# Linear attention and a leaky-ReLU MLP on one core: product 4 of the output in seven quarter products

## The chip, the cores and the metric

The kernel runs on one core of a Trainium2 chip. A core has a matrix engine (TensorE, PE in the profile; its weight loads are listed apart as PEld), a vector engine (VectorE, DVE), a scalar engine (ScalarE, ACT) and GpSimd (POOL). Transfers are issued on the queues of SP, ACT and POOL. Each engine works through its own instructions in order and waits on semaphores for the others. The metric is the device time of one execution in microseconds (us); lower is better.

## What is computed

```python
kv  = einsum('bhsd,bhse->bhde', k, v)          # 8 batches, 8 heads, 576 tokens, head size 64
out = einsum('bhsd,bhde->bhse', q, kv)
x   = out / sqrt(mean(out**2, -1) + 1e-6) * g_norm     # then (4608 tokens) x (512)
h   = x @ w_in                                  # 512 -> 2048
g   = maximum(0.01 * h, h)
y   = g @ w_out                                 # 2048 -> 512
```

All is float32. Attention is a small part of the work. The two products of the MLP are most of it.

## The kernel before

**Blocks and pieces.** The 4608 tokens are 9 blocks of 512 (`NB`, index `i`). The 2048 hidden columns are 4 pieces of 512 (`NC`, index `c`). One pair (i, c), numbered n = (i-1)*4 + c, has two parts. Its h part computes the 512 x 512 piece of h for the block, which becomes g after the leaky ReLU. Its output part multiplies this piece of g by the matching 512 rows of `w_out` and adds the result to the block's output. Block 0 is computed plainly while the weights arrive, block 1 with one level of Strassen's method (Winograd's form), and blocks 2 to 8 as follows.

**Strassen's method in short.** A product of two matrices, each cut into four quadrants, is made of 7 products instead of 8. The operands are quadrants or sums of quadrants, and the results are added up. The kernel numbers the products 1 to 7. The order is `ORDER = (1, 2, 6, 5, 7, 3, 4)`. Products 1, 6, 7 and 4 follow one another in one PSUM bank and 2 (or 5) and 3 in another, each read out before the next is added on top.

**h, two levels (`product_h_two`).** Each of the 7 outer products (j) is itself made of 7 inner products (k) of 128 x 128 quarters. A step is one k for all seven j: 4 matmuls into bank `ha` or `hc`, 3 into `hb` or `hd`. Fresh results are copied by ACT into `qa` and `qc`, others added there by DVE. The first index of `qa[:, at, j, :]` is the quadrant that k belongs to, the second the outer product j. After the seventh step DVE adds up the outer products to the quadrants g11, g21, g22, g12 with seven instructions of 128x512 (lines 960 to 970), ACT applies `relu` to each, and POOL makes the sums that the output products 5, 6, 7 and 3 need (`sums_of`, four instructions of 128x512).

**Output, one level (`product_o`).** Seven products, each of 4 matmuls of 128x256 in program order. The profile shows two matmul records for each matmul, thus 8 records of 128x256 for an output product and 2 of 128x128 for a quarter. Product 2 of the indices 4 to 29 is not made here. It is made in seven quarter products by `Second`, one in each h step of index n+2, in the free fourth column of the bank `hb` or `hd`. For these indices `product_o` runs in the order `(1, 5, 6, None, 7, 3, 4)`, where None is a slot without an output step. Results are added to the output tiles `o11`, `o12`, `o21` and `o22` by DVE, or copied by ACT at the first piece of a block (c = 0). `finish` stores a tile when its last product of the block is in it.

**Slots.** An index has seven slots, t = 0 to 6; `slot = 7*c + t` counts through a block. The main loop writes into each slot, in this order: one step of h; steps of the attention of a later block (`FINE_SLOTS`, `LATE_SLOTS`); sums of the next block's x (`sums`, by DVE, in slots 20 to 22; `inner`, by POOL, in slots 24 and 25 and after 27); loads; the inner sums of g for `Second` (`inner_g`, POOL, at t = 4 and 6); and one step of the output product. The output steps of index n run two slots late (`LAG`): from t = 2 of index n+1 to t = 1 of index n+2. Blocks 2 to 8 keep this program order on each engine (`steady`), except for the relus, copies by ACT and stores, which a planner may place.

**Weights.** The quarters of `w_in` and their sums lie in DRAM (`w1_dram`) and pass through a ring of five places (`w_place`, `RING`), one load of 448 KB per slot on SP's queue (line 742). The sums of `w_out` for products 5 and 6 (`t12`) and 7 and 4 (`t34`) are loaded by the inner function `sums` of `sides_w2` on the same queue (line 674), 512 KB each, for index n+1 as soon as index n no longer needs the place.

**Lines that recur in the profile.** L118 is every matmul. L637 is every addition by DVE or POOL (`add`). L833 is `relu`. L952 is the copy of h by ACT, L1003 the copy of an output product. L400 and L402 scale x at the end of an attention, L455 turns q.

Of the kernel before, what the change touches and what calls it, by code (L numbers as in the profile page):

```python
# [9 lines left out]
F32 = mybir.dt.float32  # L10
# [13 lines left out]
def kernel(  # L24
# [36 lines left out]
    nc = tc.nc  # L61
    B, H, S, D = q.shape
    DM, DF = w_in.shape
    P = 128
# [34 lines left out]
    NW = U * NE * P  # L99
    w1_all = consts.tile([P, 2 * NC * NW], F32, name="w1_all")  # L100
    stage = consts.tile([P, 3 * NW], F32, name="stage")
    pairs = consts.tile([P, 4 * NW], F32, name="pairs")
    g_all = [consts.tile([P, 4 * U * N2], F32, name=f"g_{i}") for i in range(2)]

    def view(t, lo, *shape):
# [79 lines left out]
    zeros = view(g_all[0], 0, NT)  # L185
    nc.vector.memset(zeros[:, :64], 0.0)
    nc.vector.memset(zeros[:, 64:], 0.0)
    ident = consts.tile([P, P], F32, name="ident")

    def make_ident():  # L190
        pin(nc.gpsimd.memset(ident, 1.0))
# [449 lines left out]
    def sides_w1(c):  # L641
# [9 lines left out]
        def more():  # L651
# [5 lines left out]

    w2_dram = [[dram.tile([P, 2, U, N2], F32, name=f"w2_{c}_{i}") for i in range(2)]
               for c in range(NC)]
    t12, t34 = pair(2, 2, U, N2), pair(3, 2, U, N2)  # L660
    writes = []

    def sides_w2(n):

        c = n % NC
        b11, b12 = w2_sb[0][c][:, :, :N2], w2_sb[0][c][:, :, N2:]
        b21, b22 = w2_sb[1][c][:, :, :N2], w2_sb[1][c][:, :, N2:]

        def sums(i):
            t = (t12, t34)[i]
            if n >= NC:
                pin(nc.sync.dma_start(t, w2_dram[c][i]))
                return
            if i == 0:
                add(nc.gpsimd, t[:, 0], b12, b11, True)
                add(nc.gpsimd, t[:, 1], b22, t[:, 0], True)
            else:
                add(nc.gpsimd, t[:, 0], b22, b12, True)  # L680
                add(nc.gpsimd, t[:, 1], b21, t12[:, 1], True)
            if (n, i) == (NC - 1, 1):

                writes.append((w2_dram[c][i], t))
            else:
                pin(nc.sync.dma_start(w2_dram[c][i], t))
        return {1: b11, 2: b21, 3: b22, 5: t12[:, 0], 6: t12[:, 1], 7: t34[:, 0],
                4: t34[:, 1]}, sums
# [49 lines left out]
    def read(to):  # L738
        nonlocal n_read
        while n_read < min(to, len(reads)):  # L740
# [5 lines left out]
    qc = pair(0, 4, 3, P)  # L746
    xt1 = [work.tile([P, 2, N2], F32, tag="xt1", name="xt1"),
           view(w1_all, RING * NG + 24 * P, 2, N2)]
    xt24 = [work.tile([P, 2, 2, N2], F32, tag="xt24", name="xt24"),
            view(w1_all, RING * NG + 16 * P, 2, 2, N2)]  # L750
    xi = view(stage, 0, 3, 7, P)

    def sides_x(i):


        x = xTs.pop(i)
        b11, b12 = x[:, :2, :N2], x[:, :2, N2:]
        b21, b22 = x[:, 2:, :N2], x[:, 2:, N2:]
        home = i % 2 if i > 1 else 0
        t1, t2, t4 = xt1[home], xt24[home][:, 0], xt24[home][:, 1]  # L760
        if i == 1:
            t4 = opool.tile([P, 2, N2], F32, tag="o", name="xt4", bufs=6)
        t3 = b12
        sides = {1: b11, 2: b21, 3: b22, 4: t4, 5: t1, 6: t2, 7: t3}

        def sums():
            for t, a, b in ((t1, b12, b11), (t2, b22, t1), (t3, b22, b12), (t4, b21, t2)):
                add(nc.vector, t, a, b, True)
                yield

        batches, quarters, at = [], {k: {} for k in ORDER}, 0
        upper, lower = (x[:, h:h + 2, :].rearrange("p r (t v n) -> p t r v n", t=2, v=2)
                        for h in (0, 2))
        for js, y in (((1, 7), upper), ((2, 3), lower),
                      ((6, 4), xt24[home].rearrange("p t r (v n) -> p t r v n", v=2)),
                      ((5,), t1.rearrange("p r (v n) -> p r v n", v=2).unsqueeze(1))):
            terms = [y[:, :, r, v, :] for r in range(2) for v in range(2)]
            terms += [xi[:, k, at:at + len(js), :] for k in range(3)]
            batches.append(terms)
            for n, j in enumerate(js):  # L780
                for k, term in zip((1, 7, 2, 3, 5, 6, 4), terms):
                    quarters[k][j] = term[:, n, :]
            at += len(js)

        def inner(kind):
            for y11, y12, y21, y22, t1, t2, t4 in batches:
                if kind == 0:
                    add(nc.gpsimd, t1, y12, y11, True)
                    add(nc.gpsimd, t2, y22, t1, True)
                elif kind == 1:  # L790
                    add(nc.gpsimd, y12, y22, y12, True)
                else:
                    add(nc.gpsimd, t4, y21, t2, True)

        return sides, quarters, sums(), inner
# [83 lines left out]

    gi = view(pairs, 12 * P, 4, P)

    def inner_w2(c):
        y = w2_sb[1][c]
# [7 lines left out]

    def inner_g(c, half):

        g = g_of(c)[3]
        a11, a21, a12, a22 = (g[:, n, :] for n in range(4))
        s1, s2, s3, s4 = (gi[:, n, :] for n in range(4))
        if half == 0:
            add(nc.gpsimd, s1, a21, a22)  # L900
            add(nc.gpsimd, s2, s1, a11, True)
        else:
            add(nc.gpsimd, s3, a11, a21, True)
            add(nc.gpsimd, s4, a12, s2, True)

    class Second:
# [17 lines left out]
        def done(self, k, bank):  # L924
# [3 lines left out]
            if self.n % NC == NC - 1 and k == ORDER[-1]:  # L928
                self.finish("11", self.o)

    def product_h_two(i, c, quarters, to, second):

        n0 = 7 * ((i - 2) * NC + c)
# [1 line left out]
        into = {1: (0, True), 2: (0, False), 6: (1, True), 5: (3, True), 7: (3, False),  # L935
                3: (1, False), 4: (2, True)}
        banks = {}
        for t, k in enumerate(ORDER):
            for js, tags, q in zip(GROUPS, (("ha", "hc"), ("hb", "hd")), (qa, qc)):
                tag = tags[0 if k in (1, 6, 7, 4) else 1]  # L940
# [14 lines left out]
                if len(js) < 4 and second:  # L955
                    second.done(k, banks[tag][:, 3, :])
            read(n0 + t + 1 + RING)
            yield
        g11, g21, g22, g12 = g_of(c)
        add(nc.vector, g21, qa[:, :, 0, :], qa[:, :, 1, :])  # L960
        add(nc.vector, g11, qa[:, :, 0, :], qc[:, :, 0, :])
        yield
        add(nc.vector, g22, g21, qa[:, :, 2, :])
        add(nc.vector, g12, g22, qa[:, :, 3, :])
        yield
        add(nc.vector, g22, g22, qc[:, :, 1, :])
        yield
        add(nc.vector, g21, g21, qc[:, :, 1, :])
        add(nc.vector, g21, g21, qc[:, :, 2, :])
        for t in (g11, g12, g22, g21):  # L970
            relu(t)
        sums_of(c, to)

    def product_o(n, g_sides, os, finish, second):

        c = n % NC
        w_sides, _ = sides_w2(n)
        sums = sides_w2(n + 1)[1] if n + 1 < NC * (NB - 1) else lambda i: None
        if c == 0:

            for key in ("12", "22", "11", "21"):
                os[key] = opool.tile([P, 2, N2], F32, tag="o", name=f"o{key}", bufs=6)


        pieces = ((0, slice(0, N2)), (1, slice(0, P)), (1, slice(P, N2))) \
            if n + 1 == NC * (NB - 1) else None
# [2 lines left out]

        def done(i, bank):  # L990
            key, fresh = into[i]
            if isinstance(bank, list):
                for at, (end, (part, cols)) in enumerate(zip(bank, pieces)):
                    to = os[key][:, part, cols]
                    add(nc.vector, to, end, to)
                    if i == ORDER[-1]:
                        finish(key, os[key], part, cols, (nc.sync, nc.scalar)[at % 2])
                if i == 7:
                    finish(key, os[key])
                return  # L1000
# [2 lines left out]
                nc.scalar.copy(to, bank)  # L1003
            else:
                add(nc.vector, to, bank, to)
            if c == NC - 1 and i in (2, 7, 3, 4):
                finish(key, os[key])

            if i == (6 if second else 5):
                sums(0)  # L1010
            elif i == 4:
                sums(1)


        yield from strassen((("oa", "oc"), ("oc", "oa"))[n % 2], lambda i, part, r: g_sides[i][:, 2 * r + part, :],
                            lambda i, part, r: w_sides[i][:, r, :], done,
                           (1, 5, 6, None, 7, 3, 4) if second else ORDER,
                           pieces=pieces)

    def go(steps, n=None):  # L1020
        while n is None or n > 0:
# [16 lines left out]
    def first_block(between):  # L1038
# [26 lines left out]
                       start=(now[2] == 0), stop=(n == 2 * NC * U))  # L1065
            between(n, 1)
        for t in range(4):
            o = opool.tile([P, DM], F32, tag="o", name="o", bufs=6)
            if t % 2:
                nc.scalar.copy(o, accs[t])  # L1070
            else:
# [35 lines left out]
    for part in range(2):  # L1107
# [4 lines left out]
    FINE_SLOTS = {1: 1, 2: 1, 4: 1, 9: 1, 10: 2, 11: 1, 12: 1, 15: 1, 16: 2, 17: 2, 18: 1, 19: 1,  # L1112
                  23: 1, 24: 1, 25: 1, 26: 1}
    LATE_SLOTS = (3, 4)

    LAG = 2

# [1 line left out]
    HELD = (22, 24, 26)  # L1119
    o_queue, waited = collections.deque(), 0  # L1120

    seconds = {}

    def second_of(n):
        if n in seconds:
# [9 lines left out]
    for i in range(1, NB):  # L1135
# [4 lines left out]
        for c in range(NC):  # L1140
# [3 lines left out]
            for t in range(7):  # L1144
                slot = 7 * c + t
                go(h_steps, 1)
                if not one:

                    if t == 6:
                        go(h_steps, 1)  # L1150
                    if slot in LATE_SLOTS:
                        go(late, 1)
                    for _ in range(FINE_SLOTS.get(slot, 0)):
# [1 line left out]
                    if i + 1 < NB:  # L1155
                        if slot == 20:
                            x_sides, new_quarters, sums, inner = sides_x(i + 1)
                        if slot in (20, 21, 22):
                            go(sums, 2 if slot == 20 else 1)
                        if slot == 24:  # L1160
                            inner(0)
                        elif slot == 25:
                            inner(1)
                    load_some()

# [1 line left out]
                if now - 1 in seconds:  # L1167
# [2 lines left out]
                            inner_g((now - 1) % NC, half)  # L1170
                    if t == 5 and now <= 2 * NC:
                        inner_w2((now - 1) % NC)
                if slot == 4 and not one:
                    while writes:
                        pin(nc.sync.dma_start(*writes.pop()))
# [32 lines left out]
            for _ in range(2 if i == NB - 1 and c == NC - 1 else 0):  # L1208
                go(h_steps, 1)
                go_o()  # L1210
            go(h_steps)
            if c == NC - 1 and i + 1 < NB:
                inner(2)
                quarters = new_quarters
# [39 lines left out]
```

## Time and profile before

| | us |
|---|---|
| median of 3 runs | 918.88 |
| runs | 918.8, 918.88, 924.28 |
| the profiled execution, device time | 917.78 |
| its span, first to last instruction | 916.1 |

| engine | what it does most | count, mean ns |
|---|---|---|
| PE | output product, 128x256, bank `o_a`, operands in `pairs` and `gs` | x384, 381 |
| PE | h, 128x128, bank `h_ha`, operands in `stage` and the weights | x448, 276 |
| DVE | output tile + bank `o_c`, 128x512 | x87, 684 |
| DVE | sum of g, 128x512 | x84, 689 |
| ACT | leaky ReLU, 128x512 | x124, 631 |
| POOL | sum of g for the output, 128x512 | x64, 1277 |
| POOL | inner sum of g, 128x128 | x52, 459 |

The mean of a matmul [...] overlaps the next one, so what a matmul costs is read from the distance between starts or from a stretch of many. DVE's instructions overlap a little in the same way. Times in a timeline are us from the start of the span. The granted clock of PE is 1.00 in every stretch.

### The profile page before, as it was taken

How to read it: one execution, taken by the hardware profiler on the slowest of the kernel's cores; microseconds unless marked ns; L12 is line 12 of the kernel's file. 1: busy time of each engine (PE TensorE's matmuls, PEld its weight loads, DVE VectorE, ACT ScalarE, POOL GpSimd, SP SyncE). 2: the span in 40 equal slices, each digit the busy share in tenths (PEclk: the TensorE clock that was granted, in tenths of full speed). 3: DMA queues.
4: the chain of work that ended last, by engine and by line, in shares of the span. 5: the costliest groups of instructions: out<-in, count | busy, mean ns of one | idle time of the engine just before them, and what ended most of it. 6: DMA issues, size and time to landing. Idle time of an engine off the chain costs nothing.

```text
span 916.1 us, 18037 instructions
## 1 busy us (share of the span) xinstructions
PE 909.3 (99%) x6980; PEld 776.3 (85%) x6980; DVE 631.6 (69%) x1168; ACT 328.2 (36%) x645; POOL 370.2 (40%) x438
## 2 busy tenths in 40 slices
PE   9999999999999999999999999999999999999998
PEld 5444448888998999899999999999999999999997
DVE  4876995587457876587756786678659755755565
ACT  5454533242135233533343324332343333223330
POOL 2000355967633473226421642264226422642222
DMA  8999926885599778776886789658765676667632
GB/s 269 236 245 249 248 85 191 280 285 167 166 360 289 228 209 268 233 230 214 255 247 230 219 249 272 222 178 212 242 183 176 187 222 198 185 185 223 197 109 92
DMA packets 90228, 200.05 MB, mean 218 GB/s; under 512 B 9888, under 2 KB 42272, under 8 KB 90144
## 3 DMA queue, kind: packets, MB, share of 16 engines
q1 hardware_dynamic: 79680, 187.04, 68.6%
q10 hardware_dynamic: 10016, 10.69, 3.4%
q8 instruction: 55, 0.90, 0.4%
q0 software_dynamic: 448, 1.18, 0.3%
q14 instruction: 29, 0.24, 0.1%
HBM read 172.39 MB, written 26.48 MB: 217 GB/s over the span
## 4 chain that ended last, share of the span: by engine, by line
PE 96%; DMA 2%; DVE 1%; issue 0%; ACT 0%; POOL 0%; SPq 0%; ACTq 0%; DVEq 0%; POOLq 0%
PE o_a L118 19%; PE o_c L118 18%; PE h_ha L118 11%; PE h_hb L118 11%; PE h_hc L118 8%; PE h_hd L118 8%; PE o_acc L118 6%; PE h_ps L118 6%; PE o_ps L118 3%; PE h_a L118 2%; PE h_b L118 1%; PE h_c L118 1%; PE h_d L118 1%; PE kv_ps L118 1%; DMA pairs<-in_v_dram 1%; DMA v_in<-in_v_dram 1%
## 5 line engine op out<-in xcount | busy, mean ns | idle before, releaser
L637 POOL TENSOR_TENSOR gs<-g 128x512 f32<-128x512 f32 x64 | 81.7, 1277 | 253.3 <-ACT g L833 253.3
L833 ACT ACTIVATE g<-g 128x512 f32<-128x512 f32 x124 | 78.2, 631 | 131.9 <-DVE g L637 131.9
L952 ACT COPY w_all<-h_ha 128x512 f32<-128x512 f32 x84 | 48.9, 582 | 173.5 <-PE h_ha L118 167.8
L118 PE MATMUL o_a<-pairs,gs 128*128 128x256 f32 x384 | 91.3, 381 | 0.0
L118 PE MATMUL o_c<-pairs,gs 128*128 128x256 f32 x376 | 89.2, 380 | 0.0
L637 DVE TENSOR_TENSOR o<-h_hb,o 128x128 f32<-128x128 f32 x104 | 29.8, 287 | 83.8 <-ACT pairs L952 83.7
L637 DVE TENSOR_TENSOR o<-o_c,o 128x512 f32<-128x512 f32 (+1 forms) x91 | 61.2, 672 | 23.9 <-PE o_c L118 23.6
L118 PEld LDWEIGHTS o_a<-pairs,gs 128*128 128x128 f32 x384 | 69.8, 190 | 9.2 <-POOL pairs L637 1.2
L118 PEld LDWEIGHTS o_c<-pairs,gs 128*128 128x128 f32 x376 | 68.3, 190 | 7.6
L637 DVE TENSOR_TENSOR o<-o_a,o 128x512 f32<-128x512 f32 x75 | 51.2, 683 | 28.2 <-PE o_a L118 28.1
L637 POOL TENSOR_TENSOR pairs<-w_all 128x512 f32<-128x512 f32 x8 | 11.1, 1384 | 120.6 <-ACT cut L245 102.3
L118 PE MATMUL h_ha<-stage,w_all 128*128 128x128 f32 x448 | 59.6, 276 | 0.0
L118 PEld LDWEIGHTS h_ha<-stage,w_all 128*128 128x128 f32 x448 | 56.6, 192 | 3.0 <-issue 0.7
L118 PE MATMUL h_ps<-xT,w_all 128*128 128x512 f32 (+1 forms) x136 | 58.0, 570 | 0.9 <-DVE w_all L258 0.9
L118 PE MATMUL o_acc<-w,g 128*128 128x512 f32 x128 | 57.8, 595 | 0.0
L637 DVE TENSOR_TENSOR g<-g,pairs 128x512 f32<-128x512 f32 x84 | 55.7, 689 | 1.9
L637 POOL TENSOR_TENSOR pairs<-g 128x128 f32<-128x128 f32 x52 | 23.9, 459 | 75.4 <-PE h_hb L118 46.7
L118 PEld LDWEIGHTS h_ps<-xT,w_all 128*128 128x128 f32 x136 | 25.5, 190 | 30.0 <-issue 26.6
L637 DVE TENSOR_TENSOR w_all<-h_hc,w_all 128x512 f32<-128x512 f32 x56 | 38.3, 684 | 15.9 <-PE h_hc L118 15.8
L118 PEld LDWEIGHTS o_acc<-w,g 128*128 128x128 f32 x128 | 24.0, 190 | 29.8 <-issue 29.4
L637 DVE TENSOR_TENSOR o<-h_hd,o 128x128 f32<-128x128 f32 x78 | 22.1, 283 | 37.8 <-ACT pairs L952 37.7
L118 PE MATMUL h_hb<-stage,w_all 128*128 128x128 f32 x336 | 46.7, 275 | 0.0
(228 smaller groups left out, 2264.6 us busy)
## 6 DMA issues: line engine op xcount, KB each, us to landing
w_all<-w SPq DMA_DIRECT2D x196, 448.0 KB, 4.2
pairs<-w SPq DMA_DIRECT2D x56, 512.0 KB, 4.3
out_dram<-o ACTq DMA_DIRECT2D x35, 256.0 KB, 4.6
v_in<-in_v_dram SPq DMA_DIRECT2D x29, 288.0 KB, 5.7
k_in<-in_k_dram SPq DMA_DIRECT2D x28, 288.0 KB, 5.1
q_in<-in_q_dram SPq DMA_DIRECT2D x56, 144.0 KB, 6.0
q_in<-in_q_dram SPq DMA_DIRECT2D x56, 140.0 KB, 5.8
w<-stage SPq DMA_DIRECT2D x12, 512.0 KB, 4.6
```

Source lines behind the costliest of these rows:

```text
L118: pin(nc.tensor.matmul(*args, **kw))
L637: ins = eng.tensor_tensor(out_, a, b_, op=ALU.subtract if minus else ALU.add)
L833: nc.scalar.activation(t, t if src is None else src, func=AF.Prelu, alpha=SLOPE)
L952: nc.scalar.copy(q[:, at], bank)
```

## The change

Product 4 of the output is made in seven quarter products for the indices n = 8 to 28 (`four(n)`), by a new class `Fourth`:

- `Fourth` makes its quarters in four steps at t = 1, 2, 3 and 4 of index n+2, right after the step of h: (1, 2, 5), (6, 3), (7) and (4). They go into three columns of the PSUM bank in which products 1, 6 and 7 of n were. Each quarter result is added to `o21` by DVE, or copied by ACT where it is the first of a block.
- Its operands are quarters of `w_out` sums that POOL makes once in block 2 (`inner_w4`) and that go to DRAM (`w4_dram`); for each index 256 KB and 192 KB are loaded in place of 256 KB. `inner_g` makes the inner sums for g12 (product 2) and g22 (product 4) together, 256 columns wide in place of 128.
- `product_o` of these indices runs in the order `(1, None, 6, 5, 7, 3, None)`. Product 7 goes to an output tile of its own ("7"), which is added to `o22` and to `o21` at the end of a block.
- The sums of g are made first for quadrant 0 (after the fourth step of h, at t = 3), the rest after the last step: four instructions at t = 6, and three with the relus and POOL's sums after the next index's first step of h (`h_rest`).
- The sums of x run in slots 20, 22, 23 and 25, one each, and POOL's inner sums of x in slots 26 and 27 and after.
- The tiles: `pairs` grows by 4*128 columns; the output tiles have 4 buffers, and 2 for `o11`, in place of 6; `ident` lies in the place of a later tile.

```diff
+        def sums(i, row=None):
             t = (t12, t34)[i]
+            if n >= NC and i:
+                if row != 1:
+                    pin(nc.sync.dma_start(t[:, 0], w2_dram[c][i][:, 0]))
+                if row == 0:
+                    return
+                if not four(n):
+                    pin(nc.sync.dma_start(t[:, 1], w2_dram[c][i][:, 1]))
+                    return
+                pin(nc.sync.dma_start(f4, w4_dram[c][:, :4, :]))
+                pin(nc.sync.dma_start(f4_more, w4_dram[c][:, 4:, :]))
+                return
...
+    class Fourth:
+        STEPS = (1, 2, 5), (6, 3), (7,), (4,)
+        COLUMN = {1: 0, 6: 0, 7: 0, 4: 0, 2: 1, 5: 2, 3: 2}
...
+        def step(self, at):
+            if at == 0:
+                self.bank = ps_m.tile([P, 4, P], F32, tag=self.tag, name=f"f_{self.tag}")
+            for k in self.STEPS[at]:
+                matmul(self.bank[:, self.COLUMN[k], :], lhsT=self.left[k], rhs=self.right[k],
+                       start=(k == 1), stop=True, skip_group_check=True)
+            for k in self.STEPS[at]:
+                bank = self.bank[:, self.COLUMN[k], :]
+                v, s = INTO[k]
+                to = self.o_of("21")[:, v, s * P:s * P + P]
+                if self.n % NC == 0 and k in (1, 5, 6, 4):
+                    nc.scalar.copy(to, bank)
+                else:
+                    add(nc.vector, to, bank, to)
+            if at == 3:
+                self.last()
...
+        def add_up(lo, hi):
+            g11, g21, g22, g12 = (g[:, lo:hi, :] for g in g_of(c))
+            a, b = qa[:, lo:hi], qc[:, lo:hi]
+            add(nc.vector, g21, a[:, :, 0, :], a[:, :, 1, :])
+            add(nc.vector, g11, a[:, :, 0, :], b[:, :, 0, :])
+            yield
+            add(nc.vector, g22, g21, a[:, :, 2, :])
+            add(nc.vector, g12, g22, a[:, :, 3, :])
+            yield
+            add(nc.vector, g22, g22, b[:, :, 1, :])
+            yield
+            add(nc.vector, g21, g21, b[:, :, 1, :])
+            add(nc.vector, g21, g21, b[:, :, 2, :])
...
             read(n0 + t + 1 + RING)
+            if t == 3:
+                for _ in add_up(0, 1):
+                    pass
             yield
...
+        for _ in add_up(1, 4):
+            yield
+        for g in g_of(c):
+            relu(g)
         sums_of(c, to)
...
+            if fourth and i == 7:
+                if c == NC - 1 or not four(n + 1):
+                    add(nc.vector, os["22"], os["22"], os["7"])
+                if c == NC - 1:
+                    finish("22", os["22"])
...
+            elif i == 4 and NC <= n < 2 * NC:
+                inner_w4()
+                later.extend(([3, lambda: (
+                    pin(nc.sync.dma_start(w4_dram[c][:, :4, :], f4)),
+                    pin(nc.sync.dma_start(w4_dram[c][:, 4:, :], f4_more)))],
+                    [4, lambda: sums(1, 1)]))
...
+        def last():
+            sums(1, 1)
+            if c == NC - 1 or not four(n + 1):
+                add(nc.vector, os["21"], os["21"], os["7"])
...
+        if fourth or four(n - 1):
+            order = (1, None, 6, 5, 7, 3, None if fourth else 4)
+        elif second:
+            order = (1, 5, 6, None, 7, 3, 4)
...
                     if t == 6:
-                        go(h_steps, 1)
+                        go(h_steps, 1 if (i, c) == (NB - 1, NC - 1) else 2)
+                    if t in FOURTH_AT and four((i - 1) * NC + c - 2):
+                        fourths[(i - 1) * NC + c - 2].step(t - FOURTH_AT[0])
+                    if t == 0:
+                        go(h_rest)
...
-                        if slot in (20, 21, 22):
-                            go(sums, 2 if slot == 20 else 1)
-                        if slot == 24:
+                        if slot in (20, 22, 23, 25):
+                            go(sums, 1)
+                        if slot == 26:
                             inner(0)
-                        elif slot == 25:
+                        elif slot == 27:
                             inner(1)
```

## The prediction

> **What bounds the kernel now.** I read the page's busy shares and its chain first. The chain is the work that ended last, followed back to the start.
>
> ```profile
> PE 909.3 (99%) x6980; PEld 776.3 (85%) x6980; DVE 631.6 (69%) x1168; ACT 328.2 (36%) x645; POOL 370.2 (40%) x438
> ...
> PE 96%; DMA 2%; DVE 1%; issue 0%; ACT 0%; POOL 0%; SPq 0%; ACTq 0%; DVEq 0%; POOLq 0%
> ```
>
> TensorE (PE) is never idle and is the chain. The time can fall only if PE has less to do, and it rises by whatever makes PE wait. Next come the stretches of one index n = (i-1)*4 + c (seven slots). The columns are stretch, length, then busy time of PE, PEld, DVE, ACT and POOL.
>
> ```profile
> 592.40:617.58 25.18, 25.18 (x250) 23.02 (x248) 20.33 (x39) 9.52 (x19) 15.30 (x20) 1.00 0.62 189
> 617.58:640.45 22.87, 22.87 (x162) 21.63 (x161) 18.91 (x34) 6.46 (x12) 10.23 (x12) 1.00 0.80 210
> ...
> 734.92:757.79 22.87, 22.87 (x162) 21.63 (x161) 11.59 (x24) 8.22 (x15) 6.83 (x8) 1.00 0.72 219
> ...
> 780.65:803.92 23.27, 23.13 (x161) 21.70 (x160) 17.13 (x31) 6.46 (x12) 15.07 (x20) 1.00 0.61 185
> ```
>
> These are n=19 (c=3), 20 (c=0), 25 and 27. A piece takes 22.87 us of pure PE work, more where attention adds matmuls. VectorE (DVE) fills 81-83% of a c=3 and a c=0 piece, but only half of n=25. Only n=27 loses something, 0.4 us. Two slots of n=20 price the matmuls:
>
> ```profile
> 631.63:635.14 3.51, 3.51 (x25) 3.31 (x24) 3.48 (x7) 0.00 (x0) 1.73 (x2) 1.00 0.92 189
> 635.14:636.93 1.79, 1.79 (x17) 1.78 (x16) 1.79 (x3) 0.00 (x0) 0.00 (x0) 1.00 1.05 340
> ```
>
> The second has only a step of h: 8 quarter products (16 records of 128x128), 1.79 us, so 0.224 us per quarter. The first has an output step besides, so a product of 8 records of 128x256 costs 3.51 - 1.79 = 1.72; the chain lists them at 1.73.
>
> [...] Here 1.73/8 = 0.216 against 1.79/16 = 0.112 us, 1.93: [...] so halving the width is nearly free and 7 for 8 is kept.
> [...] The trace has 689 and 283-287. Cutting one instruction in two costs DVE a fixed part.
> [...] POOL's 1.27 us sum from 599.03 holds a sum of x to 1.28, where 0.68 is usual, and POOL's next takes 1.61.
>
> ```profile
> 599.56 1.28 DVE L637 TENSOR_TENSOR xT<-xT 128x512 f32<-128x512 f32 x1
> ```
>
> **The change part by part.**
>
> *Product 4 (n = 8 to 28: 21 times).* Four matmuls of 128x256 go (1.73 us), seven quarters come (7 x 0.224 = 1.57). PE saves 0.16 x 21 = **3.4 us**. This is on the path.
>
> *Their evictions.* One DVE add of 128x512 becomes seven of 128x128. DVE starts back to back at these distances in n=20:
>
> ```profile
> 623.95 0.68 DVE L637 TENSOR_TENSOR o<-o_c,o 128x512 f32<-128x512 f32 x1
> 624.55 0.68 DVE L637 TENSOR_TENSOR w_all<-h_hc,w_all 128x512 f32<-128x512 f32 x1
> 625.15 0.55 DVE L637 TENSOR_TENSOR pairs<-h_hd,pairs 128x384 f32<-128x384 f32 x1
> 625.61 0.28 DVE L637 TENSOR_TENSOR o<-h_hd,o 128x128 f32<-128x128 f32 x1
> 625.81 1.25 DVE L455 STREAM_TRANSPOSE qT<-q_in 128x576 f32<-128x576 f32 x1
> ```
>
> That is 0.60, 0.46 and 0.20 us for 512, 384 and 128. So 7 x 0.20 - 0.60 = +0.8 us of DVE per index. Where n%4 is 0, four of them are ACT copies; ACT is 28-44% busy in these pieces and hides them. Product 7 now goes to a tile of its own, and two adds of 128x512 per block join it to 22 and 21: 2 x 0.69[...]. The stores of 22 and 21, issued on ACT's queue, wait for them, and ACT's copies of the next h stand behind; as the stores waited for DVE before, I add nothing. The output tiles have four and two buffers instead of six; each is written again four slots or more after its store is issued, and stores land in 4.6 us: nothing. Nor for the identity's new home, whose last reader is done in the first attention.
>
> *Sums of g (n = 4 to 31).* Seven instructions become 7 of a quarter (at t=3) and 7 of three quarters: +0.07 each by the distances, up to +0.15 where each waits for the last (the last three of an index take 2.02, 0.67 each). Total +0.5 to +1.1 per index. Four run at t=6, three behind the copies of the next t=0, with the relus behind them. The first sum on POOL then starts some 5.5 us into the index against 5.8 before (623.42 - 617.58). Product 6 needs the second at 13.95, by slot lengths below; POOL has it near 8. That costs nothing: some 5 us of margin, and at c=0 still 2 if POOL is held up.
>
> *POOL.* The inner sums of g are 256 wide instead of 128: 0.74 for 0.46 us (rows of 128x256 and 128x128), so +1.1 per index. POOL has over 10 us idle in an index, except at c=3, where the inner sums of x (8 us from 606.2 to 614.2) now move two slots later, into the time of the sums of g. In block 2, 16 sums of w2 (0.46 each, 7.4 us in all) fall into the same idle time.
>
> *DMA.* Each fourth product reads 192 KB more (448 instead of 256), block 2 writes 448 KB four times: 6 MB on 200 MB, beside engines 58-88% busy in these pieces. Landing takes 4.3 us; the data are asked for at t=4 and used at t=1 of the next index, some 14 us later. On SP the loads wait for the last quarter at t=4. Behind them stand the second load and the ring of first-layer weights, five slots deep, so 4 us of delay is hidden; without that cover a slot would wait up to 4 us. In block 2 a load waits for the write issued one slot earlier: 4 to 5 us against the four slots to its use. Bound 0 to 4 us in all; I take 0.
>
> *Sums of x* in slots 20, 22, 23, 25 instead of 20, 20, 21, 22. This takes the delay out of n=27, whose 0.4 us come from this queue (PE there waits for an eviction behind it): **-0.4**.
>
> *The new wait.* Product 5 at t=5 starts in the bank where the quarters of the former index end at t=4; it must wait for the eviction of the last one. That eviction stands on DVE behind everything of t=3 and t=4. Behind product 5 on PE stands the whole h of t=6. The slots are now 3.51, 2.46, 3.96, 2.01, 3.74 us (1.79, plus 1.73 where an output step is left, plus 0.224 per quarter), so PE reaches product 5 at 15.68 + 1.79 = 17.47 us of the index. DVE finished the evictions of h in slot t=4 of n=20 at 634.45, 16.9 us in. To that come: seven quarters +1.4; the seven quarter sums +1.8; the earlier sums shorter, -0.95; no output eviction at t=3, -0.6; idle gaps of 1.06 and 1.17 us that can be used, 0 to -2.2; and waits for POOL in the seven larger sums, which now meet POOL's sums of x and g, 0 to +2.8 (0.4 each, about two thirds of the 0.6 lost at 599.56). This makes 16.35 to 21.35, so 0 to 3.9 us late. I take the middle of both open terms: 18.85, then give 0.4 back because those gaps partly grow with the waits: 18.45, **1.0 us late**. This holds for n=12, 16 and 20, with attention's transposes: 3.0 us. At n=24, without them (two of 1.1), nothing. At c=3 (n=11, 15, 19, 23) PE gets there at 19.8, as attention's 2.3 us lie before it; DVE was through at 611.5, 19.1 in, and two sums of x leave that stretch (-1.8): 17.9 to 19.9. I take 0.1 each: 0.4. Total **+3.4**. The other indices have 7 to 11 us of DVE to spare.
>
> **Sum.** 917.78 (the profiled execution: span 916.1 and 1.7 around it) - 3.4 - 0.4 + 3.4 = 917.4. The median of the runs is 1.1 above that execution, so 918.5.
>
> **The rivals.**
> *The evictions keep up* (no new wait). For it: the same DVE work has idle gaps, and the sums by quadrant free the copies of h from waiting behind relus. Against: a c=0 piece goes from 18.9 to about 21 us of DVE in 22.7. Time: 918.88 - 3.8 = 915.1. This is also nearly the most that can be won, since PE's saving is 3.4.
> *Slower: DVE sets the pace from c=3 to c=0.* Place: the bank of product 5. All waits for POOL occur and no gap is used: 3 x 3.9 at n=12, 16, 20, 1.7 at n=24 (2.2 less), 0.6 at each of four c=3: 15.8 us. Time: 918.9 - 3.8 + 15.8 = 931. It decides from 13 us of waiting on, that is 1.9 us in each of the seven laden pieces.
> *The saving isn't there*, because short runs of one to three quarters between wide products cost extra. Against: the number of changes between widths does not grow (an output step fewer per index), and slots with and without an output step differ by just 1.72. It would add 3.4: 922.
>
> **How the numbers follow.** Waits of 2 to 7 us (917 to 922; the likeliest): 0.44. Evictions keep up: 0.26. DVE sets the pace: 0.22, of which 0.16 lies above 928. Saving missing or DMA late in block 2 (920 to 926): 0.08. The range 914.5 to 929 leaves out some 0.05 below and 0.15 above. Within 1% (9.2 us, about what a measurement can tell here) lies nearly all of this: faster by more 0.02, since no part can give 9 us; slower by more 0.17.
>
> **What would show it.** Product 4 gone from the wide groups: 168 fewer of 128x256 records (21 x 8) and 294 more of 128x128. Light pieces (n=25, 26) at 22.7 us. DVE near 21 us in c=0. PE's weight loads waiting for a DVE add "o" ahead of product 5 in c=0. I'd be wrong if light pieces aren't shorter, if PE waits for POOL's sums or for DMA, or if it waits for evictions of h.

## The result, and the profile after

| | before | changed |
|---|---|---|
| median, us | 918.84 (918.02 to 924.28) | 975.22 (971.18 to 977.13, 4 runs) |
| ratio to before | | 1.0594 [1.0541, 1.0648] |
| the profiled execution, us | 917.78, span 916.1 | 976.23, span 974.5 |

The changed kernel is 56 us slower. The page's busy times and its chain, after:

```profile
PE 920.6 (94%) x7106; PEld 784.9 (81%) x7106; DVE 713.4 (73%) x1478; ACT 335.6 (34%) x669; POOL 414.8 (43%) x454
...
PE 72%; DMA 11%; DVE 10%; issue 2%; ACT 2%; POOL 1%; SPq 1%; DVEq 0%; ACTq 0%; POOLq 0%
```

PE was busy for 99% of the span and is now busy for 94%. DVE's share of the chain goes from 1% to 10%. DMA's 11% are 107 us, of which 93 lie in the first 230 us: PE waits for a load of `v_in` at 90.4 and again at 172.6, and the chain, followed back from there, runs through the loads beside PE. The stretches of n=19, 20, 25 and 27, columns as before:

```profile
619.94:650.10 30.16, 26.95 (x256) 24.47 (x255) 23.87 (x52) 9.74 (x19) 16.06 (x20) 0.94 0.50 150
650.10:676.27 26.17, 23.23 (x167) 21.82 (x166) 23.11 (x47) 6.53 (x12) 12.26 (x13) 1.00 0.71 212
779.92:804.69 24.77, 22.97 (x167) 21.75 (x166) 15.31 (x39) 8.32 (x15) 7.98 (x8) 1.00 0.69 211
829.46:855.64 26.18, 22.97 (x167) 21.75 (x166) 20.72 (x44) 6.57 (x12) 17.25 (x21) 1.00 0.56 171
```

All four are longer, even n=25, where DVE is busy for only 15.3 of 24.8 us. That speaks against DVE's total work as the cause and for the place of something in DVE's order; the experiments below test it. In n=19 the granted clock is 0.94. What PE waits for, in the list of waits (total us, times, longest):

```profile
PE f_oc L118 <- DVE o L638: 23.3, 9, 3.2
...
PE f_oa L118 <- DVE o L638: 17.1, 13, 1.8
```

`f_oa` and `f_oc` are the banks of `Fourth`: PE waits before quarter products, for an eviction of a quarter product (L638 is `add` in the changed kernel). Of these waits 18 stand before quarter product 4, which reads `pairs` and `g`. (The list puts one of them, at 585.05, down to a load of `q_in`, which this matmul doesn't read; the eviction of the quarter ends at 584.99, and the wait is as long as its neighbours, 1.80 us.) The timeline of a light piece, n=26, around one of them (start, duration, engine, line, what; the wait in brackets):

```profile
816.41 0.39 PE L118 MATMUL f_oa<-stage,pairs 128*128 128x128 f32 x2
...
817.33 0.28 DVE L638 TENSOR_TENSOR g<-w_all 128x128 f32<-128x128 f32 x1
...
817.53 0.82 DVE L638 TENSOR_TENSOR g<-w_all,pairs 128x128 f32<-128x128 f32 x1
...
818.27 0.60 DVE L638 TENSOR_TENSOR g<-g,w_all 128x128 f32<-128x128 f32 x2
...
818.90 1.22 DVE L638 TENSOR_TENSOR g<-g,pairs 128x128 f32<-128x128 f32 x3
820.04 0.28 DVE L638 TENSOR_TENSOR o<-f_oa,o 128x128 f32<-128x128 f32 x1
...
820.38 0.49 PE L118 MATMUL f_oa<-pairs,g 128*128 128x128 f32 x2 [1.80 <-DVE o L638]
```

The first line is quarter product 7, in slot t=3. Its eviction, `o<-f_oa`, comes only at 820.04: the seven quarter sums of g stand ahead of it on DVE, from 817.33 to 820.12. Quarter product 4 is added into the same column of the bank, so it can't start before that eviction. Between the two PE has one step of h, 1.79 us, because slot t=3 has no output step any more. The rest is a wait of 1.80 us. Two of the seven sums last long: 0.82 us for the usual 0.28 while POOL's inner sum of g at 817.46 runs, and 0.70 (the first of the three from 818.90) beside the next one. At c=3 the same place is worse (n=11):

```profile
422.01 0.77 POOL L638 TENSOR_TENSOR stage<-xT 128x256 f32<-128x256 f32 x1
...
422.12 1.61 DVE L638 TENSOR_TENSOR g<-g,w_all 128x128 f32<-128x128 f32 x2
...
423.76 1.63 DVE L638 TENSOR_TENSOR g<-g,pairs 128x128 f32<-128x128 f32 x3
...
425.65 0.79 PE L118 MATMUL f_oc<-pairs,g 128*128 128x128 f32 x2 [3.21 <-DVE o L638]
```

Two quarter sums that took 0.60 us in the light piece take 1.61 beside POOL's inner sums of x; one by one, five of the seven now last 0.70 to 0.82 us. The seven run from 421.18 to 425.39, and PE waits 3.21 us.

The whole difference of the two spans, 58.4 us, by place. PE's idle stretches are counted one by one in the trace; the rows on starting again and on half clock are estimates from the lengths of pieces:

| | us |
|---|---|
| before quarter product 4: 5 x 3.21 (c=3), 12 x 1.80, one of 0.18 | 37.9 |
| before quarter products 6 and 3, at c=0, 0.37 to 1.51 each | 4.3 |
| start again after a wait: n=25 is 2.07 longer than the 22.70 it takes without the wait, of which 1.80 is idle; 0.27 x 23 | 6.2 |
| half clock after a wait, in n=11, 15 and 19: PE's busy time beyond that of the same pieces without it | 6.0 |
| n=6, 7 and 8, where the quarter sums delay evictions of h and of output products | 4.0 |
| the start: n=4 begins at 232.18 instead of 228.41 | 3.8 |
| saved matmul time, 21 x 0.165 | -3.5 |
| sum | 58.7 |

The indices 10, 14 and 18 show no wait: attention's matmuls lie between the quarter products 7 and 4 there. They are 0.16 us shorter than before.

### The profile page after: what moved, and what is told of

It reads as the page before. It is cut to its first block, busy times and chain, and to the rows that moved or that the text cites. A ratio compares the mean times of both kernels' runs of the same rounds, so it can differ in the third digit from the quotient of the medians.

```text
span 974.5 us, 18747 instructions
## 1 busy us (share of the span) xinstructions
PE 920.6 (94%) x7106; PEld 784.9 (81%) x7106; DVE 713.4 (73%) x1478; ACT 335.6 (34%) x669; POOL 414.8 (43%) x454
## 4 chain that ended last, share of the span: by engine, by line
PE 72%; DMA 11%; DVE 10%; issue 2%; ACT 2%; POOL 1%; SPq 1%; DVEq 0%; ACTq 0%; POOLq 0%
PE o_a L118 14%; PE o_c L118 14%; PE h_ha L118 7%; PE h_hc L118 7%; PE h_hb L118 7%; DVE g L638 7%; PE h_hd L118 7%; PE o_acc L118 3%; DMA stage<-in_moe_w_in_dram 3%; DMA v_in<-in_v_dram 2%; PE o_ps L118 2%; PE h_ps L118 2%; DVE o L638 2%; DMA pairs<-in_moe_w_in_dram 2%; DMA q_in<-in_q_dram 2%
## 5 line engine op out<-in xcount | busy, mean ns | idle before, releaser
L638 POOL TENSOR_TENSOR gs<-g 128x512 f32<-128x512 f32 x64 | 84.1, 1314 | 240.5 <-ACT g L852 238.4
L118 PE MATMUL o_a<-pairs,gs 128*128 128x256 f32 x384 | 95.0, 392 | 0.7 <-issue 0.7
L638 DVE TENSOR_TENSOR o<-h_hb,o 128x128 f32<-128x128 f32 x104 | 29.7, 286 | 82.4 <-ACT pairs L1028 79.8
L638 DVE TENSOR_TENSOR g<-g,pairs 128x128 f32<-128x128 f32 (+1 forms) x168 | 79.4, 499 | 2.9
L118 PEld LDWEIGHTS o_a<-pairs,gs 128*128 128x128 f32 x384 | 72.5, 198 | 9.9 <-issue 0.8
L638 DVE TENSOR_TENSOR o<-o_c,o 128x512 f32<-128x512 f32 (+1 forms) x81 | 54.4, 671 | 27.0 <-PE o_c L118 26.9
L638 POOL TENSOR_TENSOR pairs<-w_all 128x512 f32<-128x512 f32 x8 | 11.3, 1415 | 125.5 <-DMA stage<-in_moe_w_in_dram 95.8
L638 POOL TENSOR_TENSOR pairs<-g 128x256 f32<-128x256 f32 x52 | 39.5, 759 | 55.5 <-PE h_hd L118 38.6
L638 DVE TENSOR_TENSOR g<-g,w_all 128x128 f32<-128x128 f32 (+1 forms) x112 | 61.0, 544 | 2.1
L118 PE MATMUL o_acc<-w,g 128*128 128x512 f32 x128 | 58.7, 603 | 0.0
L638 DVE TENSOR_TENSOR o<-o_a,o 128x512 f32<-128x512 f32 x64 | 43.8, 684 | 19.6 <-PE o_a L118 19.2
L638 POOL TENSOR_TENSOR pairs<-g,pairs 128x256 f32<-128x256 f32 x26 | 20.7, 795 | 79.3 <-PE h_hd L118 79.3
L638 DVE TENSOR_TENSOR o<-h_hd,o 128x128 f32<-128x128 f32 x78 | 22.1, 283 | 41.8 <-ACT pairs L1028 41.8
```

What stands on the lines that cost most here:

```text
L118: pin(nc.tensor.matmul(*args, **kw))
L638: ins = eng.tensor_tensor(out_, a, b_, op=ALU.subtract if minus else ALU.add)
```

## The experiments

All compute everything, and each ratio is to the kernel before on the same chip. Theory A at first: the loss is the place of the quarter sums on DVE, ahead of the eviction that quarter product 4 needs.

**1. The quarter sums two slots later.**

```diff
-            if t == 3:
+            if t == 5:
                 for _ in add_up(0, 1):
```

> The seven sums of quadrant 0 of g move from slot t=3 to slot t=5, behind the last eviction of the quarter products; nothing else changes. Theory A (order on DVE: in slot 3 the quarter sums stand ahead of the eviction of quarter product 7, and quarter product 4, one step of h later, adds into the same PSUM column and so waits for it): the 38 us of PE idle time before quarter product 4 go, and with them the 5 to 7 us of half clock that follow the longest of them; 925 to 935 us, with some 4 us of waits left before products 6 and 3 at c=0. Theory B (DVE has too much to do in all; where the sums stand does not matter): the waits appear elsewhere, 955 to 975 us.

Measured: 932.8 us, 1.0152 [1.0119, 1.0185]. One number in the program takes 42 us away, three quarters of the loss, and every wait before quarter product 4 is gone. The light pieces n=25 and 26 are 22.70 us long, just what the saving promises (22.87 - 0.17). What is left are mainly five waits before quarter products 6 and 3 at c=0 (1.3 to 2.1 us):

```profile
PE f_oa L118 <- DVE o L638: 9.4, 5, 2.1
```

Besides, PE waits 3.9 us for `v_in` at the start, n=4 begins 5.4 us later than before, and three steps of h at c=0 wait 0.2 to 0.6 us.

**2. No quarter products of product 4, the sums of g as changed.** `four(n)` returns False.

> Product 4 is made whole again for every index; the sums of g by quadrant, the sums of x in four slots, the wider inner sums of g and the smaller output buffers stay. Theory A: without the quarter products nobody waits for the evictions behind the quarter sums, so 916 to 923 us, like the kernel before. Theory B (the split sums themselves are too much for DVE): 935 to 960 us.

Measured: 936.67 us, 1.0202 [1.0162, 1.0242]. A missed. The kernel loses 18 us with no `Fourth` at all; how much of this is the slot of the quarter sums, experiment 6 tells. The chain of this kernel, n=11 (start, duration, engine and what):

```profile
424.07 0.91 DVE g L638 x2
...
425.01 0.70 DVE g L638
...
425.71 0.43 DVE turned L383
...
426.65 0.60 DVE o L638
427.25 0.61 DVE w_all L638
427.86 0.04 issue
427.90 1.16 PE h_ha L118 x8
```

Behind the quarter sums stand attention's step, the eviction of an output product and that of h, and the next step of h waits for the last, 0.15 us here; the output product after it waits another 0.80 for the eviction of the product before. Such pairs of waits stand at c=3 in four blocks, and single ones of 0.5 to 1.1 us at c=0. So the sums delay whatever comes behind them on DVE; quarter product 4 is only the first to feel it.

**3. The quarter step ahead of the quarter sums, in the same slot.** The sums of t=3 are held back until the eviction of quarter product 7 has been issued.

```diff
-                for _ in add_up(0, 1):
-                    pass
+                held.append(add_up(0, 1))
...
                         fourths[(i - 1) * NC + c - 2].step(t - FOURTH_AT[0])
+                    while held:
+                        for _ in held.pop():
+                            pass
```

> The quarter sums of g stay in slot t=3 but are written behind the step of quarter product 7, so that its eviction stands ahead of them on DVE. Theory A: the wait before quarter product 4 goes as in the move to slot 5; DVE is then late for the eviction of quarter product 4 itself, which product 5 needs a slot later; 922 to 938 us. Theory B: as the DVE work of the slot is the same, at least 955 us.

Measured: 951.53 us, 1.0362 [1.0331, 1.0393]. It lies between the two: half of A's gain came. The waits before quarter product 4 vanish, and PE waits elsewhere:

```profile
PE f_oa L118 <- DVE o L638: 9.2, 5, 2.1
PE o_c L118 <- DVE o L638: 9.2, 6, 2.2
...
PE o_a L118 <- DVE o L638: 4.7, 4, 1.5
```

`f_oa` are quarter products 6 and 3 at c=0, with 1.4 to 2.1 us each (0.4 to 1.5 in the changed kernel). `o_c` and `o_a` are product 5, the place that the prediction named. It waits 0.9 to 2.2 us at c=3 and 0.9 to 1.5 at c=0.

**4. The sums of g whole, at the end of the index, the quarter products kept.** `add_up(0, 4)` after the last step of h; none in slot t=3.

> The quarter products of product 4 stay, but the sums of g are made whole (seven of 128x512) after the last step of h, as in the kernel before. Theory A: nothing stands ahead of the eviction of quarter product 7 in slot 3; 916 to 930 us, with waits left at c=0, where the sums of g and the copies of h run into products 6 and 3 of the quarter products. Theory B (total DVE work, here 0.5 to 1.1 us less per index than after the change): 940 to 960 us.

Measured: 946.47 us, 1.0301 [1.0269, 1.0333]. A missed again: nothing waits before quarter product 4, but the step of 6 and 3, at t=2, waits in c=3, c=0 and c=1:

```profile
PE f_oc L118 <- DVE o L638: 12.3, 10, 1.3
...
PE f_oa L118 <- DVE o L638: 6.3, 5, 1.4
```

The evictions of quarter products 1 and 5, at t=1, now stand behind DVE's end-of-index sums, and 6 and 3 go into the same columns. ACT has a part in it: at n=13 the sums end at 461.1, then DVE is idle for 1.06 us until ACT, held up by the relus of these sums, has copied h out of bank `hb`, and the evictions come only at 464.2. So a whole set of sums is too late for t=2, and an early one at t=3 too early for t=4. The theory widens: every step of `Fourth` waits for the eviction of the one before it, and DVE work ahead of that eviction costs PE time as soon as it is longer than the PE work between the two. (Of the 28 us that this kernel loses in its profile, 6 lie at the start.)

**5. As 1, with the sums of x, and POOL's inner sums of x, in the slots they had before.**

```diff
-                        if slot in (20, 22, 23, 25):
-                            go(sums, 1)
-                        if slot == 26:
+                        if slot in (20, 21, 22):
+                            go(sums, 2 if slot == 20 else 1)
+                        if slot == 24:
                             inner(0)
-                        elif slot == 27:
+                        elif slot == 25:
                             inner(1)
```

> As the run with the quarter sums of g in slot 5, and besides the sums of x (slots 20, 20, 21, 22) and POOL's inner sums of x (slots 24, 25) stand where they stood before the change. Theory A2 (the 2 us before quarter products 6 and 3 at c=0 come from the sums of g at the end of c=3 and POOL's inner sums of x, moved into the same time[...]): the five waits at c=0 shrink from 1.3-2.1 to below 0.5 us each and the time is 920 to 927 us. Theory B2 (DVE is late at c=0 by its own work, seven evictions and attention's transposes): the waits stay at 1.3 us or more, 930 to 936 us; or, as the sums of x are back in the crowded slots 20 to 22, new waits come at c=3.

Measured: 929.59 us, 1.0118 [1.007, 1.0166]. The waits at c=0 before 6 and 3 fall from 1.3 to 2.1 us to 0.38 (four of them) and 1.07, so the new slots of these sums had made most of them; which of the two kinds of sums, this run doesn't part. The waits before steps of h at c=0 grow, to 0.8 to 1.1 us in four pieces, and waits of 0.3 to 0.4 us before 6 and 3 appear at c=3. The time lies between the two forecasts, and its interval overlaps that of experiment 1, so it is the waits that tell the two apart.

**6. As 1, without `Fourth`.** Sums of g split at t=5, product 4 whole.

> Quarter sums of g in slot 5, product 4 whole for every index. Against the run without quarter products and with the quarter sums in slot 3 (936.7 us) it shows what the place of the quarter sums costs by itself; against the run with quarter products and the sums in slot 5 (932.8 us) what the quarter products bring or cost. Theory A: the place was what cost, so 916 to 922 us here, and the quarter products then cost about 10 us at c=0 and bring 3.4. Theory B (the split sums take too much of DVE wherever they stand): 928 to 938 us.

Measured: 927.25 us, 1.0073 [1.0032, 1.0114]. Against experiment 2 (936.67) the slot of the quarter sums alone is worth 9.4 us; each of the two intervals is some 4 us wide either way. Against experiment 1 (932.8) the quarter products cost 5.5 us more than they save. Even so 8.6 us stay lost against the kernel before. In the profile they are waits of 0.3 to 1.5 us before the first step of h at c=0, for an eviction that stands behind the quarter sums of c=3, 2.5 us at the start, and 1.8 us at n=10, where a load of `w_out` sums lands late. With the quarter sums at c=0 and c=1 alone these waits at c=0 are gone (experiment 10).

**7. Only quarter product 4 moved, behind the output step of its slot.**

```diff
-                    if t in FOURTH_AT and four((i - 1) * NC + c - 2):
+                    if t in FOURTH_AT[:3] and four((i - 1) * NC + c - 2):
...
+                if t == FOURTH_AT[3] and four((i - 1) * NC + c - 2):
+                    fourths[(i - 1) * NC + c - 2].step(3)
```

> The changed kernel with one thing moved: quarter product 4 of the step at t=4 is written behind the output step of that slot (1.73 us of PE) instead of ahead of it. DVE has the same work in the same order up to there. Theory A (PE waits at quarter product 4 for one eviction that is 1.8 us late in light pieces and 3.2 us in c=3): the light pieces lose nothing or 0.1 us there, c=3 about 1.5 us, and 25 to 40 us of the 56 come back: 933 to 950 us, with product 5 (1.8 us later, same bank) as the next to wait. Theory B (DVE's total): PE only waits at another place, 960 to 975 us.

Measured: 972.9 us, 1.0584 [1.0556, 1.0612]: nothing gained in the sum. The time is B's, not A's. In the light pieces A's forecast holds (n=25: 23.04 us for 24.77), and so it does for quarter product 4 at c=3, which still waits 1.5 us. But at c=3 and c=0 the wait goes one step on, to product 5. (The start of this execution is 3.1 us longer than in the changed kernel's profile, too.) B's reason, DVE's total, does not fit: experiment 1 has the same DVE work and takes 40 us less. The timeline at n=12:

```profile
460.29 0.68 DVE L638 TENSOR_TENSOR o<-o_c,o 128x512 f32<-128x512 f32 x1
460.89 0.27 DVE L638 TENSOR_TENSOR o<-f_oa,o 128x128 f32<-128x128 f32 x1
...
461.22 2.08 PE L118 MATMUL o_a<-pairs,gs 128*128 128x256 f32 x4 [2.40 <-DVE o L638]
```

Quarter product 4's eviction (`o<-f_oa`) now stands behind product 6's (`o<-o_c`), and product 5, in the bank of the quarters, waits for it: 2.4 to 3.5 us at c=0 and 2.3 to 3.1 at c=3, in four blocks each; in the last block 0.4 us at c=3 and nothing at c=0.

**8. Splitting less.** As 5, but nothing at t=5. At t=6 DVE makes the first four sums whole and the last three for quadrant 0, at the next t=0 the last three for the rest: 10 instructions of DVE in place of 14.

> From the version with the quarter sums in slot 5 and the sums of x as before: no sums ahead of the last step of h; at t=6 the first four sums whole and the last three for quadrant 0, at t=0 the last three for the other quadrants (ten instructions instead of fourteen). Theory A: DVE has 1.3 us less per index and nothing stands ahead of the last evictions of h; the waits at c=0 before bank h_hb (0.2 to 1.1 us) go, those before quarter products 6 and 3 stay below 0.4: 916 to 924 us. If the waits at c=0 come from the sums at t=6 and t=0 themselves, they grow: 926 to 932 us.

Measured: 941.48 us, 1.026 [1.0233, 1.0286], beyond both forecasts. Fewer instructions, more waiting:

```profile
PE f_oc L118 <- DVE o L638: 10.9, 10, 1.7
...
PE f_oa L118 <- DVE o L638: 7.2, 5, 1.5
```

These are again 6 and 3 at t=2, behind the sums of g of t=6 and t=0, as in experiment 4, and at c=3 behind the sums of x as well. DVE's number of instructions does not decide; which instruction stands ahead of which eviction does.

**9. The kernel before, profiled again,** to see whether it waits at the start as the changed kernels do.

> The kernel before, profiled again beside the others. In the profile of the changed kernel PE waits 1.8 us at 90 us for a load of v and runs 3.4 us at half clock, in a part that the change leaves as it was. If that is a matter of the execution (how fast the transfers land), it shows here too, in a size of 0 to 4 us; if it belongs to the change, PE does not wait there here. Time 917 to 920 us.

Measured: 919.53 us in ten executions. The one with a profile is the shortest, 918.0 us, with a span of 916.3 and no wait at 90 us. Four of the ten took 921.2 to 925.1 us at a mean granted clock of 0.996 to 0.999; there is no trace of these, so whether PE waits at the start in them is not known.

**10. The change where DVE has room, and only there.** Quarters of product 4 only for those n whose quarters fall into c=1 and c=2, early sums only at c=0 and c=1 and at t=5, the rest whole, the sums of x as before.

```diff
-        return 2 * NC <= n < NC * (NB - 1) - 3
+        return 2 * NC <= n < NC * (NB - 1) - 3 and n % NC in (0, NC - 1)
...
-            if t == 5:
+            if t == 5 and c < 2:
...
-        for _ in add_up(1, 4):
+        for _ in add_up(1 if c < 2 else 0, 4):
...
-            if c == 0 and fresh:
+            if fresh and (c == 0 or key == "7" and not four(n - 1)):
```

(The last line: product 7 of an index whose forerunner has no quarters begins its own tile, so it is copied there.)

> Product 4 in quarters only for the indices whose quarters are made in pieces c=1 and c=2 (n = 8, 11, 12, 15, 16, 19, 20, 23, 24, 27, 28: 11 of 21), the early sums of g at t=5 and only in pieces c=0 and c=1, everything at c=2 and c=3 summed whole at the end; sums of x where they were before the change. Theory A (all that the change loses is DVE's order around the quarters, and it loses it in the laden pieces c=3 and c=0): the pieces c=1 and c=2 stay at or near the pure PE work of the quarters (22.70 us at n=25 and 26), c=3 and c=0 return to within 0.3 us of the kernel before, PE's waits for output tiles over the whole run come to under 3 us, and the time is 916 to 921 us, the start's wait for v_in included (0 to 3 us). Theory B (the quarter sums and the wider inner sums cost wherever they stand, or product 4's extra loads do): waits of 0.3 to 1.5 us remain at c=0 as they do with the sums in slot 5 everywhere, and the time is 923 to 930 us.

Measured: 917.89 us, 0.9995 [0.9975, 1.0015] in 14 runs: no difference from before, and A's numbers in the trace. The same four pieces, n=19, 20, 25 and 27:

```profile
593.09:618.27 25.18, 25.18 (x249) 23.03 (x248) 20.32 (x39) 9.51 (x19) 16.31 (x20) 1.00 0.59 175
618.27:641.14 22.87, 22.87 (x162) 21.64 (x160) 20.28 (x41) 6.45 (x12) 11.09 (x12) 1.00 0.80 225
735.29:757.99 22.70, 22.70 (x168) 21.68 (x166) 14.60 (x39) 8.84 (x16) 7.90 (x8) 1.00 0.73 228
780.69:803.89 23.20, 23.13 (x162) 21.71 (x160) 17.12 (x31) 6.45 (x12) 16.16 (x20) 1.00 0.61 186
```

PE does not wait for an eviction of a quarter anywhere. From n=4 to n=30 the kernel is 1.8 us shorter than before (642.3 for 644.1): ten pieces by 0.16 each, n=10 and 27 by 0.07. The start is 1.4 us longer and the last index 0.3, so the spans are 916.0 and 916.1. Even kept whole the saving is 0.2% of the time, less than a measurement here can tell.

## Why the prediction was wrong

- **Product 4's matmuls**: right. 3.4 us were predicted for 21 indices, 0.16 each; the light pieces of experiments 1 and 10 are 0.17 shorter, and n=10, 14 and 18 of the changed kernel 0.16. The records have changed as forecast, 168 fewer of 128x256 and 294 more of 128x128. The rival that the saving isn't there falls.
- **The new wait**: the step that failed. The prediction held product 5 for the only matmul that would wait for an eviction of the quarters, and gave it 3.4 us; the waits between the steps of `Fourth` it put at nothing, without a reason. But inside `Fourth` products 1, 6, 7 and 4 follow one another in one column, each read out before the next. So every one of its steps waits for the eviction of the one before, as `COLUMN` and the order of the steps show. The wait before quarter product 4 costs 37.9 us, and it comes in light pieces too, where the prediction counted "7 to 11 us of DVE to spare"; n=25, which was to be 22.7 us long, takes 24.77. Spare time elsewhere in a piece does not help an eviction that has 1.79 us. Product 5 itself waits as foreseen as soon as quarter product 4 does not take the delay first: 0.9 to 2.2 us in experiment 3, up to 3.5 in experiment 7.
- **The seven quarter sums at 1.8 us**: right for DVE by itself, mis-sized for want of POOL. In the trace a sum starts 0.20 us after one that it doesn't depend on and 0.31 to 0.33 after one that works on the same part of g; over the seven that comes to 1.8. But from the first sum to the start of the eviction behind them it takes 2.7 us in the light piece and 4.1 at c=3: beside POOL a sum takes 0.70 to 0.82 us for 0.28, two of seven in the light piece (1.0 us more) and five at c=3 (2.4 more). The prediction gave such waits for POOL to the sums of three quarters at the end of the index and left them out here. The price was also put on the wrong event: added to a path of 17 us, when it stands whole ahead of an eviction due in 1.79. In the light piece the sums and the eviction end at 820.32, and PE, through with its step of h at 818.59, waits for that.
- **Sums of x**: -0.4 at n=27 was right (22.70 us in experiment 1, with the new slots; 23.20 in experiment 10, with the old). That the new slots, with POOL's inner sums of x moved along, cost something at c=0 was not seen: experiment 5, with the old slots, has waits of 0.38 to 1.07 us there where experiment 1 has 1.3 to 2.1.
- **Evictions of product 4, POOL, DMA, stores at no cost**: on the whole right, for PE's idle stretches in the changed kernel hold nothing of note for a weight load after the start, and no wait over 0.34 us for POOL's sums. (Experiments 2 and 6 each have one wait for a load of `w_out` sums, at n=10, of 1.4 and 1.8 us.) POOL's cost comes through DVE: its inner sums hold up the quarter sums.
- **The rivals**: "DVE sets the pace from c=3 to c=0", 931 us, had the side right and the place wrong: of the 21 pieces with quarters of product 4, 18 wait before quarter product 4, laden or not. One of the prediction's signs of being wrong came as well: at n=6 and 8 PE waits for evictions of h, 0.3 and 0.5 us.
- **Restart and half clock**: not foreseen, 12 us together by the estimates above. A wait cost PE more than its length: at n=25 2.07 us for 1.80 of idle time.
- **The start**: the 0.5 to 6.9 us that the changed kernels lose there (3.8 in the change itself) stay open. PE waits for `v_in` at some 90 or 170 us in eight of the ten, up to 3.9 us in experiment 1; experiments 2 and 8, with the same tiles, have no such wait, and the kernel before had none over 0.4 us in either profile. Whether this belongs to the change or to the single execution is not shown. Moving the tiles alone was not tried.

## What to carry to other kernels

When products are added one on top of another in one PSUM column with a read-out between, treat each read-out as having a due time: the PE work that lies between the two matmuls. Before moving vector work earlier, write down for every eviction behind it how much PE work covers it; a few small instructions ahead of an eviction with 1.79 us of cover cost here, in each turn, all of their length that the cover did not take (1.8 us of 2.7 in a light piece), however idle the engine was on average. Price a run of vector additions together with what GpSimd does in the same slot: the seven sums here took 2.7 or 4.1 us, where 1.8 was the price without it.

## What the runs showed of the hardware

**Half clock after some waits.** The stretches of 1 us at n=24 of experiment 1, after a wait of 2.09 us that ended at 736.2 (columns as in the other stretches: PE's busy time and its matmuls come after the length, the granted clock is the third from the end):

```profile
735.00:736.00 1.00, 0.00 (x0) 0.00 (x0) 0.96 (x5) 0.04 (x1) 0.92 (x2) 1.00 0.79 233
736.00:737.00 1.00, 0.84 (x6) 0.82 (x7) 0.39 (x3) 0.00 (x0) 1.00 (x2) 1.00 0.48 194
737.00:738.00 1.00, 1.00 (x5) 0.79 (x4) 0.49 (x2) 0.00 (x0) 1.00 (x1) 0.62 0.00 0
738.00:739.00 1.00, 1.00 (x4) 0.81 (x3) 0.00 (x0) 0.00 (x0) 1.00 (x2) 0.50 0.00 0
```

PE is granted half its clock for 3.4 us, from 737.25 to 740.66; in the changed kernel an output product after the wait at n=15 takes 3.41 us for the usual 1.73. There three of the five waits of 3.21 us came with half clock, for 3.4, 6.8 and 3.4 us (425.25 to 428.67, 531.07 to 537.89 and 640.29 to 643.71). At n=11 and 15 it began 0.40 and 0.95 us before the wait's end, at n=19 0.94 us after it. Two such waits, at n=23 and n=27, and the twelve of 1.80 us were spared. At the start 1.76 us of waiting for `v_in`, up to 90.42, came with half clock from 90.75 to 94.16. So the length of a wait alone does not tell, and what else decides was not shown.

**Vector instructions that follow one another.** In these traces additions of 128x128 that don't depend on one another last 0.28 us and start 0.20 apart, so they overlap by 0.08; where one works on the last one's result the starts are 0.31 to 0.33 apart, over half as much again. Additions of 128x512 last 0.68 to 0.69 us (the prediction's 689 ns, beside 283 to 287 for 128x128) and start 0.60 apart in the kernel before.
